# Storing only the inner sums of the nested second product's weights

## Chip, cores and metric

The kernel runs on one core of one Trainium2 chip. The metric is the device time of one execution in microseconds (us), lower is better. All data is fp32. Five engines work side by side, each through its own instructions in order: TensorE (PE, matmuls), VectorE (DVE), ScalarE (ACT), GpSimd (POOL) and SyncE (SP), which here only issues transfers (DMAs).

## The reference, cut

```python
# q, k, v: (4, 8, 768, 64); lam: (8,); domain_probs: (3072, 4); w1: (4, 512, 1024); w2: (4, 1024, 512)
for b in range(12):                       # blocks of 64 positions, per batch and head
    intra = (qb @ kb.T * Dmask) @ vb      # Dmask[i, j] = lam ** (i - j) for i >= j
    out[b] = intra + (qb * lam_pow) @ kv_state
    kv_state = lam_block * kv_state + (kb * rev_pow).T @ vb
x = out.transpose(0, 2, 1, 3).reshape(3072, 512)
p = domain_probs / (domain_probs.sum(-1, keepdims=True) + 1e-09)
y = sum(p[:, e:e+1] * (relu(x @ w1[e]) @ w2[e]) for e in range(4))
```

A block-wise decayed linear attention makes `x`; then four experts, each two matrix products with a relu between them, weighted by a gate per token.

## The kernel before

The 3072 tokens are cut into three groups of 1024, and a unit is one expert on one group. Unit order: group 0 with experts 0, 1, 2, 3, then groups 1 and 2 with experts 2, 3, 0, 1 each, so twelve units, numbered 0 to 11.

Each of the two products of a unit is done by a Strassen-like scheme of 2 x 2 blocks with seven products M1 to M7. A product's operand is a plain block of the weights (A11, A12, A22 for M1, M2, M4) or a sum of blocks (S1 to S4 for M5, M6, M7, M3). The first product of units 1 to 11, and the second product of units 4 to 11, are *nested*: each of the seven products is itself cut in 2 x 2 and done with seven inner products, whose operands are again three plain quarters (A11, A12, A22) and four inner sums (S3, S2, S1, S4). The second products of units 0 to 3 are plain, as is unit 0's first. The loop body of unit k runs the second product of unit k beside the first product of unit k + 1, piece by piece; units 4 to 11 are called the nested units.

Weights are prepared while the products run. `prepare_w1` and `prepare_w2` return lists of small jobs, *chores*: load blocks of the weights (`block`), form an outer sum on POOL (`total`, two 128x512 operations, stored to DRAM as `w2_sums`), form the four inner sums of one operand on POOL (`inner`, `inner_w2`, four 128x256 operations, tile `ops`) and store the operand to DRAM (`w1_ops`, `w2_ops`). For w2 this is done either together with the outer sums (`prepare_w2(e, both=True)`, experts 2 and 3) or later by `prepare_w2_ops(e)` (experts 0 and 1), which fetches an operand back (`w2f`), sums and stores. `w2_ops[e, m]` holds seven 256-wide entries an operand: A11, S3, S2, A22, S1, A12, S4. Six stores write them (L339). `feed3` (L1124) loads them for the product, in four loads of 256, 256, 256 and 128 KB into a ring of six `w2t` tiles; in the last unit one 896 KB load an operand goes to a tile `w2s`.

The order of everything is written out when the program is made. A count of steps `now` advances by one for each of eight parts of a product; `pump` takes the next chore when a modelled POOL is free (`free`, `busy`), with a factor PACE per unit between the chores; stores of results are held back by `store` for two steps after the modelled end of the sums, and put on SP. Until unit 4 begins, chores use tiles of a ring of seven `stage` tiles (tag "st"); at the start of unit 4 all chores that are left are forced out in one go:

```python
        if at == NEST:
            while chores:
                pump(force=True)
            chores.extend(prepare_w2_ops(0) + prepare_w2_ops(1))
            spare.append(True)
```

All else goes over the same engines in the same order lists: the attention of groups 1 and 2 runs inside units 0 to 3 (`turn`, `scores`, `values`). `values` gathers x in pairs of tiles `xc` (from the ring `small` of 42 tiles of 128x512, which also gives `m`, `to`, `gb`, `kv`, `st` and others, in turn). `pair_sums` forms four sums of them on POOL (tile `to`, L102) and SP stores both to `x_blocks` (L788 to L791). `x_fill` (L386) loads these as `xs`, the moving operand of the first product. `feed` loads that product's weights `ws_in` (L928 to L930, L932). For the last third of the attention, q and k are turned by 128 small DRAM-to-DRAM copies of 32 KB (`across`, L435), trickled out one by one on SP; before a batch is loaded back (`qx`, `kx`, L451), all its remaining copies are issued at once. `w2t` loads of the plain second products are at L1051; TensorE's matmuls are at L1018 (first product), L1072 (plain second) and L1362 (nested second); `out` stores of group 0 are at L1092. Nearly all DVE and POOL additions go through one helper, L102.

Places in the program are given below by *matmul numbers*: how many 128x256 matmuls stand ahead in TensorE's order. Unit 0 begins at 112, units 1, 2, 3 at 322, 532, 742, and unit 4 at 952. The profile records each such matmul as two.

Of the kernel before, what the change touches and what calls it, by code (L numbers as in the profile page):

```python
# [21 lines left out]
def kernel(  # L22
# [69 lines left out]
    def small(name):  # L92
        return pool.tile([P, W], FP32, name=name, tag="t")

    def acc_tile(name):
        return opool.tile([P, W], FP32, name=name, tag="acc")

# [64 lines left out]
    w1_ops = dram.tile([E, 7, P, 7, 256], FP32, name="w1_ops")  # L162
    x_blocks = dram.tile([NG - 1, P, 4, 7, 256], FP32, name="x_blocks")
    w2_sums = dram.tile([E, 4, P, 4, DH], FP32, name="w2_sums")
    w2_ops = dram.tile([E, 7, P, 7, 2, P], FP32, name="w2_ops")

    W1_AT = {n: i for i, n in enumerate(("M1", "M7", "M6", "M5", "M3", "M2", "M4"))}
    X_AT = {"M1": 0, "M5": 1, "M2": 2, "M3": 3, "M7": 4, "M6": 5, "M4": 6}
# [7 lines left out]
    def store(f):  # L176
        queue.append((busy[0] + (8 if spare else 2), f))
# [152 lines left out]
    def inner_w2(e, m, blk, two):  # L330
        b = {f"A{i + 1}{j + 1}": blk[j][:, :, i * P:(i + 1) * P] for i in range(2) for j in range(2)}
        s = [x.rearrange("p c d -> p (c d)").rearrange("p (k c d) -> p k c d", k=2, c=2) for x in two("ops")]
        for name, x, y, op in S_OPS:
            b[name] = s[SLOT[name] // 2][:, SLOT[name] % 2]
            tt(nc.gpsimd, b[name], b[x], b[y], op)
        to = w2_ops[e, MS.index(m)]
        b["S3"] = s[0]
        at = (("A11", 0), ("S3", slice(1, 3)), ("A22", 3), ("S1", 4), ("A12", 5), ("S4", 6))
        store(lambda: ([nc.sync.dma_start(out=to[:, x], in_=b[n]) for n, x in at], made.add(("w2", e, m))))  # L339

    def prepare_w2_ops(e):

        def two(name):
            return [small(name)[:].rearrange("p (c d) -> p c d", c=2) for _ in range(2)]

        st = {}

        def fetch(m):
            st[m] = two("w2f")
            for x in range(2):  # L350
                nc.sync.dma_start(out=st[m][x], in_=w2_form(e, A_OF[m])[:, 2 * x:2 * x + 2])

        def ready(m):
            inner_w2(e, m, st.pop(m), two)

        return [
            lambda: fetch(SEQ3[0]), pause(4),
            *(lambda i=i: (i < 6 and fetch(SEQ3[i + 1]), ready(SEQ3[i])) for i in range(7)),
        ]
# [173 lines left out]
    gate_bc = {}  # L533

    def spread_gates(g, e):
        gate_bc[unit_of[g, e]] = two = [small("gb")[:].rearrange("p (n t) -> p n t", t=P) for _ in range(2)]
        for j, t in enumerate(two):
            src = gate_rows[g - 1, 4 * j:4 * j + 4, e]
            nc.scalar.dma_start(out=t, in_=src.partition_broadcast(P))
# [239 lines left out]

    def pair_sums(g, x, o):  # L780

        s = [small("to") for _ in range(2)]
        (b12, b11), (b22, b21) = ((t[:, 0:256], t[:, 256:512]) for t in o)
        t1, t2, t3, t4 = (t[:, i * 256:(i + 1) * 256] for t in s for i in range(2))
        for to, a, b in ((t1, b12, b11), (t2, b22, t1), (t3, b22, b12), (t4, b21, t2)):
            tt(nc.gpsimd, to, a, b, ALU.subtract)
        store(lambda: (
            nc.sync.dma_start(out=x_blocks[g - 1, :, x, 0], in_=b11),  # L788
            nc.sync.dma_start(out=x_blocks[g - 1, :, x, 1:3], in_=o[1][:].rearrange("p (i t) -> p i t", i=2)),
            *(  # L790
                nc.sync.dma_start(out=x_blocks[g - 1, :, x, 3 + 2 * y:5 + 2 * y], in_=t[:].rearrange("p (i t) -> p i t", i=2))  # L791
                for y, t in enumerate(s)
            ),
            made.add(("blocks", g, x)),
        ))
# [308 lines left out]
    def feed3(e, m, k):  # L1104

        x_e = units[e][1]
        until(("w2", x_e, m))
        if e == FINAL and m != SEQ3[0]:

            if k == 0:  # L1110
                t = xp.tile([P, 7, 256], FP32, name="w2s", tag="x" + SEQ[SEQ3.index(m)])
                if (e, m) == PLAIN:
                    i, j = int(A_OF[m][1]) - 1, int(A_OF[m][2]) - 1
                    src = moe_w2[x_e, j * W:(j + 1) * W, i * DH:(i + 1) * DH]
                    nc.sync.dma_start(out=t[:, 0:4], in_=src.rearrange("(k p) d -> p k d", p=P))
                    fed3[e, m, 0] = t
                    return
                nc.sync.dma_start(out=t[:], in_=w2_ops[x_e, MS.index(m)].rearrange("p k c d -> p k (c d)"))
                for x in range(4):
                    fed3[e, m, x] = t[:, 2 * x:min(2 * x + 2, 7)]  # L1120
            return
        t = w2pool.tile([P, 2, DH], FP32, name="w2t", tag="w2")
        n = min(2, 7 - 2 * k)
        nc.sync.dma_start(  # L1124
            out=t[:, 0:n], in_=w2_ops[x_e, MS.index(m), :, 2 * k:2 * k + n].rearrange("p k c d -> p k (c d)"),
        )
        fed3[e, m, k] = t

# [94 lines left out]
    def plain_product(e, m, tags):  # L1225
        def part(dd, t):
            if t == 0:
                banks.append(bank(tags[dd], "p" + m))
            p = banks[dd]
            for q in range(2):  # L1230
                for c in range(2):
                    nc.tensor.matmul(
                        out=p[:, t * 256:(t + 1) * 256], lhsT=fed3[e, m, 0][:, 2 * q + c, dd * P:(dd + 1) * P],
                        rhs=outer[e][B_OF[m]][f"{q + 1}{t + 1}"][:, c * 256:(c + 1) * 256],
                        start=(t == 0 and q == 0 and c == 0), stop=True, skip_group_check=True,
                    )
            if t == 1:
                o = sums[m][:, 2 * dd:2 * dd + 2].rearrange("p k t -> p (k t)")
                tt(nc.vector, o, p[:], o, ALU.add)

        banks = []
        none = lambda: None
        return [f for dd in range(2) for t in range(2) for f in (lambda dd=dd, t=t: part(dd, t), none)]
# [17 lines left out]
    def turned_product(t, h, w):  # L1261
        p, o = ends[t], small("y")
        for s in range(2):
            for c in range(2):
                nc.tensor.matmul(
                    out=p[:, s * P:(s + 1) * P], lhsT=h[:, c * 256 + s * P:c * 256 + (s + 1) * P],
                    rhs=w[:, c * P:(c + 1) * P], start=False, stop=True, skip_group_check=True,
                )
        nc.scalar.copy(out=o[:, 0:256], in_=p[:, 0:256])
        i, j = RESULT[END[1]]  # L1270
        r = token(LAST, j, 2 * t)
        nc.sync.dma_start(
            out=out[r:r + 256, i * DH:i * DH + P].rearrange("(s p) d -> p s d", p=P),
            in_=o[:, 0:256].rearrange("p (s d) -> p s d", s=2),
        )
# [66 lines left out]
    def nested_product(e, m, tags):  # L1342
# [8 lines left out]

        def inner(x, i):
            if (e, m) == END and i in ("M2", "M3"):
                turned_product(("M2", "M3").index(i), b[B_OF[i]], fed3[e, m, x // 2][:, x % 2])
                return
            t = tags[0] if i in ("M1", "M6", "M5", "M3") else tags[1]
            fresh = i in ("M1", "M7", "M2")
            if fresh:
                banks[t] = bank(t, "p" + t)
            p = banks[t]  # L1360
            for c in range(2):
                nc.tensor.matmul(  # L1362
                    out=p[:, 0:256], lhsT=fed3[e, m, x // 2][:, x % 2, c * P:(c + 1) * P],
                    rhs=b[B_OF[i]][:, c * 256:(c + 1) * 256], start=(fresh and c == 0), stop=True,
                    skip_group_check=True,
                )
            at, begins = READ[i]
            o = sums[m][:, BLOCKS.index(at)]
            if begins and e in (NEST, 2 * E):
                nc.scalar.copy(out=o, in_=p[:, 0:256])  # L1370
            else:
                tt(nc.vector, o, p[:, 0:256], o, ALU.add)
            if (e, m, i) == (*END, "M5"):
                o = sums[m][:, BLOCKS.index("12")]
                tt(nc.vector, o, p[:, 0:256], o, ALU.add)
# [239 lines left out]
    for g in range(1, NG):  # L1615
        attention(g)
    steps.insert(0, (12, turn_gates))
    PACE = 1.15, 1.15, 1.4, 1.4, 1.3, 1.3, 1.3, 1.4, 1.0, 1.0, 1.0, 1.0
    first_steps = first_result()
    for at, (g, e) in enumerate(units):  # L1620
        if at == 0:
            chores.extend(prepare_w1(3) + prepare_w2(2, True) + prepare_w2(3, True) + prepare_w1(0))
        ahead = units[at + 1] if at + 1 < len(units) else None
        nested, nests = at >= NEST, ahead and at + 1 >= NEST
        if at == NEST:
            while chores:
                pump(force=True)
            chores.extend(prepare_w2_ops(0) + prepare_w2_ops(1))
            spare.append(True)
        blocks, banks = {}, {}  # L1630
        for i in range(7):
# [108 lines left out]
```

## Time and profile before

| | |
|---|---|
| median of 3 runs | 1242.48 us (1240.96 to 1244.87) |
| profiled execution | 1239.18 us, span 1237.3 us |
| mean granted TensorE clock | 0.975 of full speed |
| PE busy | 1158.7 us (94%), 7983 records |
| DVE / POOL / ACT busy | 842.6 (68%) / 826.3 (67%) / 316.2 us (26%) |
| transfers | 267.23 MB, 296153 packets, 216 GB/s over the span |
| chain that ended last | PE 77%, DVE 10%, DMA 5%, SP's queue 4%, POOL 1% |

Times within the span are counted from its first instruction. Windows give the busy microseconds of each engine inside a stretch; PEclk is the share of the clock that TensorE was granted; the DMA share is how busy the 16 DMA engines were on average. In a timeline the bracket names how long the engine had been idle before an instruction and which event ended that wait. "SPq" is SP issuing transfers, `w_ops` stands for `w1_ops` or `w2_ops`, `w_sums` for `w2_sums`.

### The profile page before, as it was taken

What the parts mean: (1) busy time and instruction counts of PE and PEld (TensorE: products, weight loads), DVE (VectorE), ACT (ScalarE), POOL (GpSimd) and SP (SyncE); (2) the same over time, 40 slices, a digit from 0 to 9 for tenths busy, and PEclk for the clock granted to TensorE, in tenths of its full rate; (3) what the DMA queues carried; (4) which work ended last, traced back from release to release, by engine and by line L of the source; (5) the groups of instructions that cost most, each with busy time, mean ns of one, the idle gap of its engine ahead of it and who ended that gap; (6) DMA issues with size and microseconds to landing.
All of it is one profiled execution on the core that took longest, in us unless ns stands there. A gap on an engine that the chain in (4) does not pass through costs nothing.

```text
span 1237.3 us, 21855 instructions
## 1 busy us (share of the span) xinstructions
PE 1158.7 (94%) x7983; PEld 998.1 (81%) x7983; DVE 842.6 (68%) x1525; ACT 316.2 (26%) x638; POOL 826.3 (67%) x768
## 2 busy tenths in 40 slices
PE   8999899999789984689899999999999999999998
PEld 7888788888667874577788888888887888888877
DVE  4688785775357643567457777788976667786785
ACT  4321122023101210112234234123234252242322
POOL 2856267758372644678669789898485585593884
PEclk9999999999889998799899999999999999999999
DMA  8876549999798985965498778885555665655562
GB/s 190 220 224 197 179 145 300 283 306 279 243 292 269 287 243 138 303 197 176 130 304 276 228 249 257 269 251 185 183 152 168 201 195 159 191 153 179 161 210 68
DMA packets 296153, 267.23 MB, mean 216 GB/s; under 512 B 140464, under 2 KB 236272, under 8 KB 296048
## 3 DMA queue, kind: packets, MB, share of 16 engines
q1 hardware_dynamic: 281088, 260.91, 68.9%
q10 hardware_dynamic: 14960, 4.94, 1.8%
q8 instruction: 64, 1.05, 0.3%
q14 instruction: 41, 0.34, 0.1%
HBM read 194.96 MB, written 75.01 MB: 218 GB/s over the span
## 4 chain that ended last, share of the span: by engine, by line
PE 77%; DVE 10%; DMA 5%; SPq 4%; POOL 1%; issue 1%; ACT 0%; ACTq 0%; DVEq 0%; POOLq 0%
PE pg L1018 33%; PE pq L1362 24%; PE q L1072 12%; DVE m L102 4%; PE pM L1464 2%; SPq L435 2%; DVE hT L102 1%; DVE sums L102 1%; DVE xs L102 1%; PE pc L1464 1%; DMA ws_in<-w_ops 1%; PE sp L676 1%; PE op L730 1%; DMA across<-in_k_dram 1%; PE op L748 1%
## 5 line engine op out<-in xcount | busy, mean ns | idle before, releaser
L1018 PE MATMUL pg<-xs,ws_in 128*128 128x256 f32 x1960 | 479.5, 385 | 20.5 <-DMA ws_in<-w_ops 11.5
L1018 PEld LDWEIGHTS pg<-xs,ws_in 128*128 128x128 f32 x1960 | 374.4, 193 | 79.7 <-issue 12.8
L102 DVE TENSOR_TENSOR m<-pg,m 128x512 f32<-128x512 f32 x451 | 307.7, 687 | 145.2 <-PE pg L1018 111.2
L102 POOL TENSOR_TENSOR m<-m,gb 128x512 f32<-128x512 f32 x128 | 167.2, 1325 | 97.5 <-ACT m L1030 71.6
L1072 PE MATMUL q<-w2t,m 128*128 128x256 f32 x896 | 220.4, 390 | 5.9 <-DVE m L102 5.9
L1072 PEld LDWEIGHTS q<-w2t,m 128*128 128x128 f32 x896 | 173.5, 195 | 31.9 <-DVE m L102 6.7
L1362 PE MATMUL pq<-acc,w2t 128*128 128x256 f32 x800 | 198.1, 381 | 0.2 <-DVE sums L102 0.2
L102 DVE TENSOR_TENSOR sums<-pq,sums 128x256 f32<-128x256 f32 x321 | 133.0, 420 | 86.1 <-PE pq L1362 74.1
L1362 PEld LDWEIGHTS pq<-acc,w2t 128*128 128x128 f32 x800 | 152.2, 191 | 22.0 <-issue 1.1
L1030 ACT ACTIVATE m<-m 128x512 f32<-128x512 f32 x132 | 83.0, 630 | 238.3 <-DVE m L102 233.1
L1089 DVE SCALAR_TENSOR_TENSOR acc<-q,gate,acc 128x256 f32<-128x256 f32 x96 | 46.2, 481 | 94.9 <-PE q L1072 94.5
L102 POOL TENSOR_TENSOR acc<-hT,hT 128x512 f32<-128x512 f32 x64 | 82.7, 1306 | 41.1 <-PE pq L1362 39.1
L1026 ACT COPY m<-pg 128x512 f32<-128x512 f32 x88 | 51.5, 586 | 173.4 <-PE pg L1018 165.2
L102 POOL TENSOR_TENSOR acc<-hT,acc 128x512 f32<-128x512 f32 x64 | 84.9, 1327 | 12.7 <-PE pq L1362 7.6
L102 DVE TENSOR_TENSOR m<-m,m 128x512 f32<-128x512 f32 x96 | 81.5, 851 | 11.9 <-DMA x_blocks<-xc 6.0
L1362 PE MATMUL pq<-hT,w2t 128*128 128x256 f32 x336 | 86.3, 379 | 0.1
L102 POOL TENSOR_TENSOR xs<-xs 128x256 f32<-128x256 f32 x40 | 31.8, 796 | 67.3 <-DMA xs<-x_blocks 64.5
L1362 PEld LDWEIGHTS pq<-hT,w2t 128*128 128x128 f32 x336 | 63.7, 190 | 9.1 <-DVE sums L102 0.5
L1362 PE MATMUL pq<-m,w2t 128*128 128x256 f32 x264 | 69.2, 385 | 1.7 <-DVE xc L102 1.6
L951 ACT COPY up<-m 128x512 f32<-128x512 f32 x56 | 32.5, 588 | 124.9 <-DVE m L102 124.7
L102 POOL TENSOR_TENSOR acc<-m,acc 128x512 f32<-128x512 f32 x44 | 57.0, 1295 | 3.2
L1362 PEld LDWEIGHTS pq<-m,w2t 128*128 128x128 f32 x264 | 50.2, 192 | 10.0 <-ACT xc L769 1.7
(143 smaller groups left out, 1336.6 us busy)
## 6 DMA issues: line engine op xcount, KB each, us to landing
w2t<-w_ops SPq DMA_DIRECT2D x150, 256.0 KB, 3.5
ws_in<-w_ops SPq DMA_DIRECT2D x40, 896.0 KB, 7.2
ws_in<-w_ops SPq DMA_DIRECT2D x30, 512.0 KB, 5.6
w_ops<-ops SPq DMA_DIRECT2D x28, 512.0 KB, 4.8
w_sums<-w2o SPq DMA_DIRECT2D x16, 512.0 KB, 4.3
w2t<-w_sums SPq DMA_DIRECT2D x32, 256.0 KB, 4.3
ws_in<-in_moe_w_dram SPq DMA_DIRECT2D x30, 256.0 KB, 5.7
w_ops<-ops SPq DMA_DIRECT2D x28, 256.0 KB, 4.4
```

Source lines behind the costliest of these rows:

```text
L102: eng.tensor_tensor(out=o, in0=a, in1=b, op=op)
L435: pieces.append((b, lambda to=to, src=src: nc.sync.dma_start(out=to, in_=src.rearrange("(t p) d -> p t d", p=32),)))
L676: nc.tensor.matmul(out=sp[r][half[x], ac * BL:(ac + 1) * BL], lhsT=hc(kT)[half[r], ac, blk[x]], rhs=hc(qT)[half[r], ac, blk[x]], start=(ac ...
L730: nc.tensor.matmul(out=op[r][half[y], cols(a, r) if x == r else apart(a)], lhsT=state[half[r], x, 2 * a + y], rhs=by_block(qs)[half[r], 2 ...
L951: nc.scalar.copy(out=there[at][:], in_=a[at][:])
L1018: nc.tensor.matmul(out=p[:, j * 256:(j + 1) * 256], lhsT=ws[i][:, j * P:(j + 1) * P], rhs=xs[i], start=(fresh and j == 0), stop=True, skip ...
L1026: nc.scalar.copy(out=new[at][:], in_=p[:])
L1030: nc.scalar.activation(out=new[at][:], in_=new[at][:], func=AF.Relu)
L1072: nc.tensor.matmul(out=p[:, s * DH:(s + 1) * DH], lhsT=h[at][:, c * 256 + s * P:c * 256 + (s + 1) * P], rhs=fed2[g, e, m][x][:, c], start= ...
L1089: nc.vector.scalar_tensor_tensor(out=o, in0=x, scalar=w, in1=o, op0=ALU.mult, op1=ALU.add)
L1362: nc.tensor.matmul(out=p[:, 0:256], lhsT=fed3[e, m, x // 2][:, x % 2, c * P:(c + 1) * P], rhs=b[B_OF[i]][:, c * 256:(c + 1) * 256], start= ...
L1464: nc.tensor.matmul(out=p[:, s * 256:(s + 1) * 256], lhsT=a[c][:, f:f + P], rhs=b[:, c, j * 256:(j + 1) * 256], start=(s == 0 and c == 0 an ...
```

## The change

1. `w2_ops` keeps only the four inner sums of an operand (S3, S2, S1, S4), written by two stores of 256 KB instead of six. `feed3` reads the plain quarters where they are: in the weights themselves, or in `w2_sums` (`w2_form`). An operand is again four loads: A11's quarter (128 KB, rows of 512 bytes), S3 with S2, A12 with A22, S1 with S4. In the last unit an operand is four loads instead of one.
2. Expert 2 loses `both=True`: its outer sums alone are prepared early, its inner sums by `prepare_w2_ops(2)`, later, from fetched operands. The chores of `prepare_w2_ops` for experts 2, 0, 1 are queued at unit 0, behind all others, and run before unit 4 as far as pacing lets them; the forced flush at unit 4 is gone.
3. Until unit 4 begins, the gate tiles `gb`, the x sums `to` and the tiles of `prepare_w2_ops` come from the `stage` ring instead of the `small` ring (`twice`).
4. PACE is 1.0 for 1.15 in units 0 and 1, and 1.3 for 1.4 in units 2 and 3.

```diff
+    def twice(name):
+        if spare:
+            return [small(name)[:] for _ in range(2)]
+        t = stage.tile([P, 2, W], FP32, name=name, tag="st")
+        return [t[:, i] for i in range(2)]
...
-    w2_ops = dram.tile([E, 7, P, 7, 2, P], FP32, name="w2_ops")
+    w2_ops = dram.tile([E, 7, P, 4, 2, P], FP32, name="w2_ops")
...
-        b["S3"] = s[0]
-        at = (("A11", 0), ("S3", slice(1, 3)), ("A22", 3), ("S1", 4), ("A12", 5), ("S4", 6))
-        store(lambda: ([nc.sync.dma_start(out=to[:, x], in_=b[n]) for n, x in at], made.add(("w2", e, m))))
+        store(lambda: ([nc.sync.dma_start(out=to[:, 2 * q:2 * q + 2], in_=s[q]) for q in range(2)], made.add(("w2", e, m))))
...
         def two(name):
-            return [small(name)[:].rearrange("p (c d) -> p c d", c=2) for _ in range(2)]
+            if spare:
+                return [small(name)[:].rearrange("p (c d) -> p c d", c=2) for _ in range(2)]
+            t = stage.tile([P, 4, DH], FP32, name=name, tag="st")
+            return [t[:, 0:2], t[:, 2:4]]
...
-        gate_bc[unit_of[g, e]] = two = [small("gb")[:].rearrange("p (n t) -> p n t", t=P) for _ in range(2)]
+        gate_bc[unit_of[g, e]] = two = [t.rearrange("p (n t) -> p n t", t=P) for t in twice("gb")]
...
-        s = [small("to") for _ in range(2)]
+        s = twice("to")
...
+        ops, form = w2_ops[x_e, MS.index(m)].rearrange("p k c d -> p k (c d)"), w2_form(x_e, A_OF[m])
...
+            pieces = t[:, 6], t[:, 0:2], t[:, 4:6], t[:, 2:4]
+            ks = range(4)
+        else:
+            t = w2pool.tile([P, 2, DH], FP32, name="w2t", tag="w2")
+            pieces = {k: t[:, 0] if k == 0 else t}
+            ks = [k]
+        for k in ks:
+            x = pieces[k]
             if k == 0:
+                x = x.rearrange("p (c d) -> p c d", c=2)
+                nc.sync.dma_start(out=x, in_=form[:, 0:2, 0:P])
+                w["M1"] = [x[:, c] for c in range(2)]
+                continue
+            nc.sync.dma_start(out=x[:], in_={1: ops[:, 0:2], 2: form[:, 2:4], 3: ops[:, 2:4]}[k])
...
-    PACE = 1.15, 1.15, 1.4, 1.4, 1.3, 1.3, 1.3, 1.4, 1.0, 1.0, 1.0, 1.0
+    PACE = 1.0, 1.0, 1.3, 1.3, 1.3, 1.3, 1.3, 1.4, 1.0, 1.0, 1.0, 1.0
...
-            chores.extend(prepare_w1(3) + prepare_w2(2, True) + prepare_w2(3, True) + prepare_w1(0))
+            chores.extend(prepare_w1(3) + prepare_w2(2) + prepare_w2(3, True) + prepare_w1(0))
+            for x in (2, 0, 1):
+                chores.extend(prepare_w2_ops(x))
...
         if at == NEST:
-            while chores:
-                pump(force=True)
-            chores.extend(prepare_w2_ops(0) + prepare_w2_ops(1))
+            assert len(chores) < 20
             spare.append(True)
```

More of the change, by code (lines that the diff above doesn't have):

```diff
@@ L790, in pair_sums @@
             *(
-                nc.sync.dma_start(out=x_blocks[g - 1, :, x, 3 + 2 * y:5 + 2 * y], in_=t[:].rearrange("p (i t) -> p i t", i=2))
+                nc.sync.dma_start(out=x_blocks[g - 1, :, x, 3 + 2 * y:5 + 2 * y], in_=t.rearrange("p (i t) -> p i t", i=2))
                 for y, t in enumerate(s)
@@ L1107, in feed3 @@
         until(("w2", x_e, m))
+        w = fed3.setdefault((e, m), {})
+        ops, form = w2_ops[x_e, MS.index(m)].rearrange("p k c d -> p k (c d)"), w2_form(x_e, A_OF[m])
         if e == FINAL and m != SEQ3[0]:
-            if k == 0:
[L1111 to L1127, printed above, removed]
+            if k:
+                return
+            t = xp.tile([P, 7, 256], FP32, name="w2s", tag="x" + SEQ[SEQ3.index(m)])
+            if (e, m) == PLAIN:
+                nc.sync.dma_start(out=t[:, 0:4], in_=form)
+                w[0] = t
+                return
@@ new lines, in feed3 @@
+            pieces = t[:, 6], t[:, 0:2], t[:, 4:6], t[:, 2:4]
[6 more added lines that the diff above has]
+            x = pieces[k]
+            if k == 0:
+                x = x.rearrange("p (c d) -> p c d", c=2)
[3 more added lines that the diff above has]
+            nc.sync.dma_start(out=x[:], in_={1: ops[:, 0:2], 2: form[:, 2:4], 3: ops[:, 2:4]}[k])
+            if k == 2:
+                w["M2"], w["M4"] = ([x[:, c, y * P:(y + 1) * P] for c in range(2)] for y in range(2))
+            else:
+                for y, i in enumerate({1: ("M7", "M6"), 3: ("M5", "M3")}[k]):
+                    w[i] = [x[:, y, c * P:(c + 1) * P] for c in range(2)]
@@ L1232, in part @@
                     nc.tensor.matmul(
-                        out=p[:, t * 256:(t + 1) * 256], lhsT=fed3[e, m, 0][:, 2 * q + c, dd * P:(dd + 1) * P],
+                        out=p[:, t * 256:(t + 1) * 256], lhsT=fed3[e, m][0][:, 2 * q + c, dd * P:(dd + 1) * P],
                         rhs=outer[e][B_OF[m]][f"{q + 1}{t + 1}"][:, c * 256:(c + 1) * 256],
@@ L1266, in turned_product @@
                     out=p[:, s * P:(s + 1) * P], lhsT=h[:, c * 256 + s * P:c * 256 + (s + 1) * P],
-                    rhs=w[:, c * P:(c + 1) * P], start=False, stop=True, skip_group_check=True,
+                    rhs=w[c], start=False, stop=True, skip_group_check=True,
                 )
@@ L1353, in inner @@
             if (e, m) == END and i in ("M2", "M3"):
-                turned_product(("M2", "M3").index(i), b[B_OF[i]], fed3[e, m, x // 2][:, x % 2])
+                turned_product(("M2", "M3").index(i), b[B_OF[i]], fed3[e, m][i])
                 return
@@ L1362, in inner @@
                 nc.tensor.matmul(
-                    out=p[:, 0:256], lhsT=fed3[e, m, x // 2][:, x % 2, c * P:(c + 1) * P],
+                    out=p[:, 0:256], lhsT=fed3[e, m][i][c],
                     rhs=b[B_OF[i]][:, c * 256:(c + 1) * 256], start=(fresh and c == 0), stop=True,
```

## Prediction

> **What bounds the kernel now.** I read the page first (engines and slices), then the table by stage, then TensorE's gaps, then what DVE and the SP queue did inside the largest gap. PE is busy 1158.7 of 1237.3 us, so at most 78.6 us of gaps can be won, and the slices say where they lie:
>
> ```profile
> PE   8999899999789984689899999999999999999998
> POOL 2856267758372644678669789898485585593884
> PEclk9999999999889998799899999999999999999999
> ```
>
> A slice is 30.9 us. PE and its clock dip together in slices 10 to 19, the second half of the plain units. The stage table (units 0, 1, 2, 3, then the nested units):
>
> ```profile
> core 0: us, PE busy (x) PEld busy (x) DVE busy (x) ACT busy (x) POOL busy (x), PEclk, DMA share, GB/s
> 88.50:194.00 105.50, 100.72 (x767) 87.00 (x767) 83.16 (x138) 19.61 (x39) 58.91 (x60) 1.00 0.58 178
> 194.00:298.00 104.00, 104.00 (x963) 90.07 (x962) 72.26 (x130) 21.80 (x48) 78.82 (x90) 1.00 0.94 294
> 298.00:411.50 113.50, 98.06 (x823) 81.78 (x822) 62.78 (x113) 16.14 (x38) 58.27 (x66) 0.92 0.88 265
> 411.50:573.00 161.50, 124.20 (x1068) 104.73 (x1067) 85.50 (x148) 21.08 (x48) 97.54 (x106) 0.89 0.74 224
> 573.00:1237.00 664.00, 648.96 (x3092) 563.64 (x3090) 481.97 (x860) 208.57 (x393) 485.71 (x405) 0.99 0.64 199
> ```
>
> Unit 1 is full. Unit 2 has 15.4 us of gaps and loses 0.08 x 98 = 7.8 us to the clock; unit 3 has 37.3 us and loses 0.11 x 124 = 13.7. The nested units have 15 us in 664, mostly the tail. So the change is decided between 298 and 600 us. TensorE's timeline there names what ended each gap (in brackets):
>
> ```profile
> 324.45 3.75 PE L1018 MATMUL pg<-xs,ws_in 128*128 128x256 f32 x8 [6.49 <-DMA ws_in<-w_ops]
> 365.17 3.78 PE L1018 MATMUL pg<-xs,ws_in 128*128 128x256 f32 x8 [4.21 <-DVE m L102]
> 381.29 2.07 PE L1072 MATMUL q<-w2t,m 128*128 128x256 f32 x4 [2.59 <-DVE m L102]
> 448.65 2.83 PE L1018 MATMUL pg<-xs,ws_in 128*128 128x256 f32 x8 [4.43 <-DMA ws_in<-w_ops]
> 502.35 0.48 PE L730 MATMUL op<-qs,kv 64*64 64x64 f32 x4 [22.82 <-DVE kv L102]
> 592.34 0.69 PE L730 MATMUL op<-qs,kv 64*64 64x64 f32 x32 [3.26 <-DVE kv L102]
> ```
>
> I call the first A, the next two B, then C and D. A and C wait for first-product weights. B and D wait for DVE, and DVE for a buffer: its own timeline, then SP's, inside D:
>
> ```profile
> 499.68 0.69 DVE L102 TENSOR_TENSOR m<-pg,m 128x512 f32<-128x512 f32 x1 [21.55 <-DMA x_blocks<-xc]
> ```
>
> ```profile
> 466.46 8.22 SPq L435 DMA_DIRECT2D across<-in_q_dram  x11
> 474.73 10.40 SPq L435 DMA_DIRECT2D across<-in_k_dram  x16
> 492.43 0.43 SPq L929 DMA_DIRECT2D ws_in<-w_ops  x1
> 493.44 0.64 SPq L788 DMA_DIRECT2D x_blocks<-xc  x1
> ```
>
> DVE wants an `m` tile whose buffer still holds `xc`; the store of `xc` stands on SP behind 27 small copies (18.6 us), then loads. Every one of these gaps goes back to SP's single queue being late, none to POOL's or DVE's total.
>
> **The change part by part.** TensorE's and ACT's orders are the same in both programs, DVE's differs in three moved steps, POOL has the same 762 operations. SP has 1045 transfers instead of 1128 (260.8 to 253.5 MB): 84 stores of plain blocks (0.47 to 0.6 us of SP each) go, 28 partial stores are merged, 14 fetches and 15 split loads are added. Expert 2's seven inner operands move from units 1 and 2 into unit 3, expert 0's seven from the nested units to the end of unit 3. Per unit, SP issues and MB: unit 1 132 and 31.6 to 132 and 32.6; unit 2 169 and 34.9 to 124 and 30.8; unit 3 140 and 28.9 to 169 and 36.0.
>
> A: the table above charges 6.49 us, the 0.99 us before it (a wait for POOL's `kn`) and slow matmuls. Eight records (four matmuls) take 1.73 us at full clock, 0.432 us a matmul; after the gap they took 3.75 and 2.75, so 3.0 us more: 10.5 in all. In the changed order that `ws_in` issue stands at matmul 540 instead of 561, 21 x 0.432 = 9.1 us earlier, and between matmuls 546 and 588 SP has 28 issues for 50. That covers the gap, but unit 1 sends 1.1 MB more into a DMA share of 0.94, so I take -8; bounds 0 and -10.5.
>
> (The Trainium skill, "TensorE: Matmul & The Clock Gate", section "The HAM clock gate", has the clock at half for one window of about 3.4 us after an idle one, which would lose 1.7 us, not the 3.0 of these rows; by it A and B are each 1.3 us smaller and the forecast 2.6 us later.)
>
> B: 4.21, 0.95 in the gaps just before and after, 2.59, and 3.2 + 1.9 us of slow matmuls: 12.8. DVE waited at matmul 629 for an `xc` store standing at 624. `to` tiles now come from the stage ring, the rotation of the 42 small buffers is slower, and the wait is at 625 to 627 for a store at 608: 17 x 0.432 = 7.3 us of lead against 2.2. I take -9; bounds 0 and -12.8.
>
> C: 4.43, 1.4 in two earlier `ws_in` waits, 2.1 slow: 7.9. The `ws_in` issue moves only from 762 to 757, but six stores ahead of it (SP 432.4 to 436.9 us) become four. -3; bounds +2 and -7.9.
>
> D: the 27 copies stay where they were, so the gap stays. What goes is DVE's wait at 834: in the new order that `m` tile waits for an old `vn`, and it is an ACT copy of the next `xc` at 836 that waits for the store. DVE's `kv` and the attention product are then done inside the gap, and PE resumes when `ws_in` (issued 492.4, median 5.6 to land) arrives, about 498.5, instead of at 505.2. Two `w2f` loads now stand ahead of it (+1.2); the store ahead of the copies that waits for POOL (2.9 us on SP) has 2.5 us less POOL work before it. -7; bounds +2 and -10 (with the 2.67 us `kx` wait at 520 that is DVE catching up).
>
> New in unit 3: between matmuls 866 and 952 POOL gets 48.2 us of work instead of 25.8 (seven groups of four 0.73 us sums of expert 0, which before waited for unit 4 or later), and SP 63 issues instead of 35. Before, that stretch lasted about 40 us (537 to 577). POOL's gates and inner sums stand behind the groups, and the first nested product waits for the last `acc` (562.5 to 565 before, needed near 574). So 9 us of slack there, 5.6 us of waits for ACT that the groups can fill, and 48.2 - 40 = 8 us too many: I take +4; bounds 0 and +22.4. Behind POOL stand the stores of those sums on SP, and behind them `ws_in` and `w2t`.
>
> Nested units: reading plain blocks in place replaces one for one (four `w2t` loads an operand, one of them in 512-byte runs); PE is full there and SP waits for PE 233 us, so loads have that much lead. POOL, at up to 24.7 of 25 us between 650 and 850, has seven groups fewer. 0; bounds -3 and +3.
>
> (Against it, "DMA: Bandwidth & Descriptors", section "Why small descriptors are slow", counts about 3 fixed cycles a packet; 512-byte instead of 2 KB runs would then cost, by estimate, 13% more engine time on 7 MB. No run here shows it, and the DMA share there is 0.64.)
>
> PACE 1.0 for 1.15 in units 0 and 1 moves chores a few matmuls forward; POOL has 17 us a unit free. 0.
>
> Sum: -8 - 9 - 3 - 7 + 4 = -23. The profiled execution took 1239.18 us (span 1237.3 + 1.9), 3.3 below the median of 1242.48. 1239.18 - 23 = 1216.2, and at the median's level 1219.5.
>
> **The rivals.** *Bandwidth, not order.* Unit 1 runs 294 GB/s at a share of 0.94, and up to matmul 546 the change moves 2.2 MB more (73.5 for 71.2): 7.6 us at that rate, nearly A's whole lead. Then A, B and C stay and only D and the late POOL work count: -3, about 1239.5. For it: the share. Against: in unit 1 PE never waited at that share.
>
> *POOL late at the end of unit 3 (slower).* Place: POOL, matmuls 866 to 952. If nothing absorbs the groups, 22.4 us show; a `ws_in` on SP behind a store that waits for POOL adds its 7.2 us landing, and the clock 3.0: +32.6 against the -27 won, +5.6, 1248. It decides once the first nested product starts over 27 us behind the weights. Against: the bounded slack above.
>
> *All of it.* If SP is never late before D and reaches the copies 5 us earlier, every bound is met without the POOL cost: about -40, 1202.
>
> That the change doesn't do what it says is ruled out by the program: the stores are gone, TensorE's order is unchanged.
>
> **How the numbers follow.** Forecast (1210 to 1230) 0.56, bandwidth 0.18, POOL late 0.14, all of it 0.12. A run of this kernel tells 0.3% (3.7 us) from no change: below 1238.8 is faster, above 1246.2 slower. Faster: 0.56 + 0.12 + half of bandwidth 0.09 + 0.01 = 0.78; same 0.10; slower 0.12. Leaving out about 0.06 below and 0.12 above gives 1203 to 1246.
>
> **What would show it.** Right: unit 2 near 100 us long with its clock above 0.97; no DVE wait for `x_blocks<-xc` over 2 us; D still there, 15 to 19 us, ended by `ws_in`; POOL over 22 of 25 us in the last 40 us of unit 3. Wrong: A still over 4 us with a DMA share at 0.95 (bandwidth); PE waiting for POOL `acc` or `m` at the first nested product by over 10 us (POOL late); D gone.

## The result, and the profile after

| | median, us | ratio to before, 95% interval |
|---|---|---|
| before | 1241.72 (4 runs, 1239.69 to 1244.87) | |
| changed | 1222.28 (4 runs, 1221.54 to 1223.5) | 0.9842 [0.9819, 0.9865] |

The change gains 19.4 us. The profiled execution took 1223.5 us (span 1221.7, mean granted clock 0.976), 15.7 less than the one of before. The forecast of 1219.5 was 2.8 us off. That closeness flatters it: several steps behind it were wrong and cancelled, and the experiments show which.

The page's slices for the changed kernel, 30.5 us each:

```profile
PE   8999898999999995786999999999999999999998
POOL 2857158777766752998679688686585584693884
PEclk9999999999999997897899999999999999999999
```

Counted from 0, the dips of PE and its clock that lay in slices 10 to 19 are gone from 10 to 14; those from slice 15 on remain. There is a new small one, the 8 in slice 6. The stage table of the changed kernel (units 0, 1, 2, 3, nested units; columns as in the prediction's table):

```profile
88.20:200.40 112.20, 103.47 (x767) 89.08 (x766) 81.32 (x138) 19.62 (x39) 62.87 (x67) 0.97 0.57 178
200.40:307.10 106.70, 105.47 (x966) 90.51 (x965) 77.70 (x130) 21.61 (x48) 81.35 (x86) 1.00 0.96 299
307.10:415.60 108.50, 105.09 (x989) 90.11 (x988) 75.88 (x130) 19.45 (x46) 74.56 (x82) 0.98 0.94 290
415.60:556.90 141.30, 108.98 (x901) 91.95 (x901) 74.56 (x131) 17.91 (x40) 96.23 (x113) 0.89 0.84 266
556.90:1221.70 664.80, 650.54 (x3089) 565.20 (x3088) 481.53 (x859) 208.60 (x393) 468.67 (x379) 0.99 0.57 180
```

One boundary in the prediction's own table was wrong: it cut between units 2 and 3 at 411.5 us, 14.7 us too early. By the first L1072 matmul of unit 3 the kernel before stands thus:

```profile
298.40:426.20 127.80, 112.36 (x989) 93.97 (x989) 72.52 (x129) 19.44 (x46) 69.26 (x79) 0.93 0.90 269
426.20:573.60 147.40, 110.10 (x902) 92.64 (x901) 76.09 (x131) 17.79 (x40) 86.78 (x92) 0.88 0.71 215
```

The two tables give the difference by unit: unit 0 +6.8 us (105.4 to 112.2), unit 1 +2.2 (104.5 to 106.7), unit 2 -19.3, unit 3 -6.1, nested units +1.1. Units 2 and 3, where the gain was expected, brought it, and units 0 and 1, priced at nothing, cost 9 us. TensorE's gaps in the changed kernel, from its timeline, answer to A to D:

```profile
197.43 1.13 PE L690 MATMUL sp<-vn,kn 64*64 64x64 f32 x32 [4.51 <-POOL kn L108]
363.93 3.11 PE L1025 MATMUL pg<-xs,ws_in 128*128 128x256 f32 x8 [2.07 <-DVE m L108]
372.40 1.13 PE L1079 MATMUL q<-w2t,m 128*128 128x256 f32 x4 [1.34 <-DVE m L108]
476.26 4.01 PE L1025 MATMUL pg<-xs,ws_in 128*128 128x256 f32 x8 [12.44 <-DMA ws_in<-in_moe_w_dram]
555.05 2.07 PE L1025 MATMUL pg<-xs,ws_in 128*128 128x256 f32 x4 [8.46 <-DVE m L108]
576.76 1.13 PE L737 MATMUL op<-qs,kv 64*64 64x64 f32 x32 [5.18 <-DVE kv L108]
```

A (324) and C (448) are gone. Of B two short waits are left. D is 12.44 us and ends with `ws_in`, as forecast. The first and the last two rows are new or larger: POOL is late there. SP inside D still stands behind the batch of small copies, with two `w2f` loads (0.98 us) between them and `ws_in`:

```profile
445.06 7.38 SPq L442 DMA_DIRECT2D across<-in_q_dram  x10
452.48 10.40 SPq L442 DMA_DIRECT2D across<-in_k_dram  x16
...
467.11 0.98 SPq L358 DMA_DIRECT2D w2f<-w_sums  x2
...
472.35 0.34 SPq L935 DMA_DIRECT2D ws_in<-in_moe_w_dram  x1
```

### The profile page after: what moved, and what is told of

It reads as the page before. It is cut to its first block, busy times and chain, and to the rows that moved or that the text cites. A ratio compares the mean times of both kernels' runs of the same rounds, so it can differ in the third digit from the quotient of the medians.

```text
span 1221.7 us, 21731 instructions
## 1 busy us (share of the span) xinstructions
PE 1157.0 (95%) x7983; PEld 998.0 (82%) x7983; DVE 845.4 (69%) x1525; ACT 316.0 (26%) x638; POOL 830.1 (68%) x768
## 4 chain that ended last, share of the span: by engine, by line
PE 47%; DVE 4%; DMA 1%; issue 0%; SPq 0%; ACT 0%; DVEq 0%
PE pq L1379 24%; PE pg L1025 22%; DVE sums L108 1%; DVE m L108 1%; DMA w2s<-w_ops 1%; DVE hT L108 1%; DVE xs L108 1%; PE pg L1379 0%; PE pM L1249 0%; PE yp L1209 0%; SPq L1139 0%; PE yp L1282 0%; DVE y L1230 0%; ACT m L1037 0%; SPq L1136 0%
## 5 line engine op out<-in xcount | busy, mean ns | idle before, releaser
L108 POOL TENSOR_TENSOR acc<-hT,acc 128x512 f32<-128x512 f32 x64 | 84.9, 1326 | 12.7 <-PE pq L1379 7.6
L108 DVE TENSOR_TENSOR m<-m,m 128x512 f32<-128x512 f32 x96 | 86.2, 901 | 3.7 <-PE q L1079 3.7
```

Source lines behind the costliest of these rows:

```text
L108: eng.tensor_tensor(out=o, in0=a, in1=b, op=op)
```

## The experiments

Theory: SP's single queue sets units 2 and 3, and the change wins by lightening and rearranging it; what it gives back comes from POOL's order, in unit 0 through PACE and at the end of unit 3 through the early operands of experts 0 and 1. Rivals: the new gaps are a by-product of SP's lateness, the ring rotation is what matters, or bytes do and not issues. Each group of four kernels has a median of before of its own, 1241.3 to 1243.0 us. Times of whole kernels are medians of four runs; the lengths of units and gaps come from one profiled execution of each.

### 1. PACE of unit 0 (changed kernel, one number)

```diff
-    PACE = 1.0, 1.0, 1.3, 1.3, ...
+    PACE = 1.15, 1.0, 1.3, 1.3, ...
```

> The changed kernel with the old PACE of 1.15 in unit 0 alone. In the changed kernel TensorE waits 4.51 us at 197 us for POOL's kn, which stands behind one more pair of w1 sums than before; unit 0 lasts 112.2 us instead of 105.4. Theory (the moved chore is the cause): the wait goes, unit 0 is back at 105 to 106 us, and the whole is 5 to 7 us faster than the changed kernel, near 1216. Rival (the time is only taken up by the next wait): the 4.5 us come back in units 1 and 2, where the DMA share is over 0.9, and the whole stays within 2 us of 1222.

Measured: 1216.53 us (1210.67 to 1218.79), 0.9775 [0.9739, 0.981], 5.8 less than the changed kernel. In the profile, which is of the fastest of the four runs, unit 0 is back at 105.4 us. Part of the cost moved on: unit 1 is 2.9 us longer, with a wait of 2.44 us for `kn`. Unit 3 is 8.7 us shorter in this execution. POOL's timelines show why. The changed kernel, then the kernel before, at the same place of the program:

```profile
193.30 2.48 POOL L108 TENSOR_TENSOR w1o<-w1o,w1b 128x512 f32<-128x512 f32 x2 [2.48 <-DMA w_ops<-w1o]
...
196.32 1.06 POOL L108 TENSOR_TENSOR kn<-kn,decay 128x512 f32<-128x512 f32 x1
```

```profile
191.19 1.06 POOL L102 TENSOR_TENSOR kn<-kn,decay 128x512 f32<-128x512 f32 x1
194.15 2.50 POOL L102 TENSOR_TENSOR w1o<-w1o,w1b 128x512 f32<-128x512 f32 x2 [1.89 <-PE pg L1018]
```

With PACE 1.0 a pair of outer sums, waiting 2.48 us for a buffer whose store is in flight, slips in ahead of `kn`, for which TensorE then waits 4.51 us. POOL is idle 49 of the 112 us of unit 0; its total says nothing here, its order does.

### 2. Experts 0 and 1 held back until unit 4

```diff
-            for x in (2, 0, 1):
-                chores.extend(prepare_w2_ops(x))
+            chores.extend(prepare_w2_ops(2))
...
-            assert len(chores) < 20
+            assert not chores
+            chores.extend(prepare_w2_ops(0) + prepare_w2_ops(1))
```

> The changed kernel with expert 0's (and 1's) inner sums queued only when unit 4 begins, as before the change; expert 2's are made as in the change. It takes seven groups of sums (about 20 us) off POOL between matmuls 866 and 952. Theory (POOL late at the end of unit 3): the 8.46 us gap at 555 us, where TensorE waits for DVE and DVE 9.4 us for POOL's m, goes and the whole is 7 to 11 us faster than the changed kernel, near 1213. Rival (the gap is the DVE chain's, POOL only fills it): the gap stays over 5 us and the whole within 3 us of 1222.

Measured: 1211.61 us (1210.62 to 1214.28), 0.974 [0.9714, 0.9766], 10.7 less. Unit 3 is 130.1 us for 141.3, the gap near 555 is gone, and the nested units are no longer for it (663.9 against 664.8). So making the seven operands of expert 0 at the end of unit 3 costs 10.7 us and buys nothing later. Not all of that need be POOL's: the edit also takes 30 of SP's 169 issues out of unit 3, and D is 9.87 us for 12.44. The chain behind the gap, DVE's timeline in the changed kernel:

```profile
553.30 1.09 DVE L108 TENSOR_TENSOR hT<-m,m 128x512 f32<-128x512 f32 x1 [9.36 <-POOL m L108]
```

and the busy time between 525 and 575 us, POOL the fifth engine of the row:

```profile
525.00:550.00 25.00, 19.11 (x188) 16.34 (x188) 11.58 (x21) 3.30 (x9) 24.30 (x28) 0.98 0.95 332
550.00:575.00 25.00, 16.53 (x108) 13.63 (x108) 19.56 (x24) 5.70 (x11) 24.53 (x19) 0.82 0.61 198
```

POOL is full for 50 us, the gates `m` queue behind `ops`, DVE behind the gates, TensorE behind DVE.

### 3. The x sums and gates back in the small ring

```diff
     def twice(name):
-        if spare:
-            return [small(name)[:] for _ in range(2)]
-        t = stage.tile([P, 2, W], FP32, name=name, tag="st")
-        return [t[:, i] for i in range(2)]
+        return [small(name)[:] for _ in range(2)]
```

> The changed kernel with the x sums and gates back in the ring of 42 small tiles; all else as changed. Theory (rotation of the ring is what took DVE's waits away in B and D): a wait of DVE for x_blocks<-xc of 10 us or more is back inside the long gap near 460 to 485 us, the gap is ended by DVE's kv and not by ws_in and is 5 to 8 us longer, B stays short since SP is earlier there; the whole is 5 to 9 us slower than the changed kernel, near 1229. Rival (SP's order alone sets the gap, DVE's wait lies inside it): within 3 us of 1222.

Measured: 1222.87 us (1221.13 to 1223.39), 0.9831 [0.9808, 0.9854]: no difference. The buffer wait came back all the same, in DVE's timeline:

```profile
476.61 0.69 DVE L105 TENSOR_TENSOR m<-pg,m 128x512 f32<-128x512 f32 x1 [17.07 <-DMA x_blocks<-xc]
```

D is 18.39 us then and named after DVE, instead of 12.44 named after `ws_in`; but units 2 and 3 take 107.0 and 140.4 us against 108.5 and 141.3. The name and length of one gap changed and the time did not: work that is not done inside the gap follows it, and the other way round. My theory of the ring rotation, worth 5 to 9 us, fell.

### 4. Copies across partitions earlier

Two more small copies per product in units 0 to 2, so that the batch of 26 ahead of D's `ws_in` goes:

```diff
                 if x % 2:
                     trickle()
+                if at in (0, 1, 2) and x in (2, 6):
+                    trickle()
```

> The changed kernel with two more of the 32 KB copies issued per product in units 0 to 2, so that 2 and not 26 stand on SP ahead of the last batch; the same copies in all. Theory (SP's queue, not DVE, POOL or bandwidth, sets D): the 12.44 us wait for ws_in at 476 us goes to under 3 us, with its slow matmuls, and the whole is 10 to 15 us faster than the changed kernel, near 1210. Rival (bandwidth): the copies' 128-byte pieces take DMA time from units 1 and 2, which are at a share of 0.91 to 1.00, and 5 us or more of new ws_in waits appear there; the whole is 0 to 8 us faster.

Measured: 1219.48 us (1217.2 to 1221.09), 0.9804 [0.978, 0.9829], only 2.8 less. D is gone and unit 3 takes 123.5 us for 141.3, which shows that the batch made it. But units 0, 1 and 2 are 2.1, 6.6 and 2.3 us longer. The theory was right about D and wrong about the whole. The rival has the size of the whole, but the new `ws_in` waits that it named did not come: there is one, of 1.51 us, in unit 2. The new wait in unit 1 is one of 2.97 us for POOL's `kn`. What makes these units longer is not shown; runs 8 and 9 take it up.

### 5 and 6. The two halves of the change, each alone

The stores: the changed kernel with the chores' order, PACE and flush of before.

```diff
-            chores.extend(prepare_w1(3) + prepare_w2(2) + prepare_w2(3, True) + prepare_w1(0))
-            for x in (2, 0, 1):
-                chores.extend(prepare_w2_ops(x))
+            chores.extend(prepare_w1(3) + prepare_w2(2, True) + prepare_w2(3, True) + prepare_w1(0))
...
-            assert len(chores) < 20
+            while chores:
+                pump(force=True)
+            chores.extend(prepare_w2_ops(0) + prepare_w2_ops(1))
...
+    PACE = 1.15, 1.15, 1.4, 1.4, ...
```

> The new operand layout alone: inner sums stored without the plain blocks and plain blocks read in place, but the order of the chores, their PACE and the flush before unit 4 are those of the kernel before (the stage tiles stay, since the small tiles cost nothing). Theory 'fewer stores': the five stores that each nested operand no longer queues on SP are what frees units 2 and 3; unit 2 falls from 127.8 us to about 110, unit 3 from 147.4 to 135-142, unit 0 stays at 105.4, and the whole is 1218-1226 us, as the changed kernel or better. Rival 'order': what frees unit 2 is that expert 2's nested operands are made later; then unit 2 stays above 120 us and the whole is 1233-1242 us. Halfway (1227-1232 us) the two share the gain.

The order: the kernel before with the opposite edit and the stage tiles, all six stores an operand kept.

> The other half alone: the order of the chores, PACE and stage tiles of the changed kernel, but every nested operand is stored whole, plain blocks too, with six stores each, as before. Theory 'fewer stores': unit 2 is freed in part, since expert 2's seven operands leave it, and the stores come back in unit 3, where they stand ahead of unit 3's weights: unit 2 112-118 us, unit 3 150-160, whole 1238-1248 us. Rival 'order': unit 2 falls to about 108 us and unit 3 to about 141, whole 1221-1230 us. Unit 0 is 112 us under both, since PACE sets it.

Measured: the stores alone 1207.79 us (1205.7 to 1209.39), 0.9743 [0.9697, 0.9789]; the order alone 1256.44 us (1255.06 to 1258.39), 1.0135 [1.0095, 1.0174]. So fewer stores win 33.5 us and the new order loses 15.1; the sum, -18.4, is close to the -19.4 of the change. The stores did better than their theory's 1218 to 1226 us; the order alone lies above both of its ranges, with unit 2 at 126.1 and unit 3 at 155.5 us. TensorE's gaps with the order alone:

```profile
325.67 1.96 PE L1027 MATMUL pg<-xs,ws_in 128*128 128x256 f32 x8 [1.76 <-DMA ws_in<-w_ops]
347.95 3.67 PE L1027 MATMUL pg<-xs,ws_in 128*128 128x256 f32 x8 [7.81 <-DMA ws_in<-w_ops]
585.31 2.07 PE L1027 MATMUL pg<-xs,ws_in 128*128 128x256 f32 x4 [18.99 <-DVE m L108]
```

A's wait of 6.49 us falls to 1.76, as the order's lead had it, and a wait of 7.81 us stands 22 us later: with the stores still there SP is late at another matmul. The last row, 18.99 us, is at the place of the rival "POOL late", priced at 22.4. But POOL is not full there: it is busy 38.4 us between 535 and 587, and in that stretch waits 5.8 us for fetched operands (`w2f`) and 6.0 us for their stores. So transfers stand behind this gap as well. With the stores alone the rows that answer to them are these; A is 4.05 us, D 10.84, the gap at the end of unit 3 absent, and unit 2 takes 114.7 us and unit 3 127.6:

```profile
322.58 3.12 PE L1025 MATMUL pg<-xs,ws_in 128*128 128x256 f32 x8 [4.05 <-DMA ws_in<-w_ops]
473.91 3.41 PE L1025 MATMUL pg<-xs,ws_in 128*128 128x256 f32 x8 [10.84 <-DMA ws_in<-in_moe_w_dram]
```

### 7. Both corrections together

The edits of 1 and 2 on the changed kernel.

> The changed kernel with the two corrections together: PACE of unit 0 back at 1.15, and the nested operands of experts 0 and 1 queued only when unit 4 begins. If the two costs are separate they add: 1222.3 - 5.8 - 10.7 = 1205.8 us, with unit 0 at 105.4 and unit 3 at 125-131. Rival: both act through the same reserve, how far POOL is behind as unit 3 ends; alone the first already cut the gap there from 8.5 to 4.9 us, so together they give only some 12 us: 1209-1211 us.

Measured: 1209.58 us (1209.27 to 1210.06), 0.9755 [0.9712, 0.9798]. That is 12.7 us together, not 16.5, and in the rival's range. That a POOL less far behind and a POOL with less to do are partly the same slack fits, but is not shown: run 1 alone spread over 8.1 us, so the plain sum is not excluded. What is left of the new order, expert 2's operands made later and the PACE of units 1 to 3, is worth nothing over the stores alone: 1209.6 against 1207.8, unit 1 longer (110.4 us for 104.5), unit 2 shorter (109.1 for 114.7). In unit 1, where PACE is still 1.0, POOL again forms a pair of w1 sums ahead of `kn`, after 6.29 us of waiting for a buffer, and TensorE waits 3.23 us for `kn`. That wait is absent in the stores alone (PACE 1.15) and in the changed kernel (1.0 in both units). No run changes PACE in unit 1 alone, so its cause stays open.

### 8, 9 and 10. Copies earlier where the DMA engines are free

Two more copies per product in unit 0 alone (DMA share 0.57), on top of 7, then on top of the stores alone; the third, also on the stores alone, has four more per product in place of two.

```diff
+                if at == 0 and x in (2, 6):      # third: (0, 2, 4, 6)
+                    trickle()
```

> The same with 14 extra copies of q and k across partitions in unit 0 alone, where the DMA engines are busy 57% of the time against 95% in units 1 and 2, so that some 12 of 26 copies are left in the batch ahead of unit 3's weights. Theory (SP's queue sets the gap near 476 us, and the extra copies cost time only where the DMA engines are full): the gap falls by 12-14 x 0.6 us, some 6 us, units 1 and 2 stay within 1 us of the run without the copies, and the whole is 4-6 us below that run, about 1200 us. Rival (a copy costs what it saves wherever it stands): unit 0 or 1 is longer by as much, and the whole is within 2 us of the run without the copies.

> The new operand layout alone (old order and PACE, 1207.8 us) with the 14 extra copies of q and k in unit 0. Theory: the 10.84 us gap ended by ws_in near 474 us goes, with the slow matmuls behind it, as it did on top of the other version (-12.2 us there): 1195-1198 us. Rival: in the old order the copies meet other stores in unit 2 (114.7 us, DMA engines 93% busy) and come out even: 1204-1208 us.

> The same with 28 extra copies in unit 0, so that no batch is left. Theory: once the gap is gone there is nothing more to win in unit 3; units 1 and 2 are as with 14: within 2 us of that run. Rival: each copy taken out of units 1 and 2 frees 0.6 us of SP there and shortens the rest of the wait at 322 us (4.05 us) and the one at 370 us: 3-6 us less.

Measured: 1197.39 us (1194.78 to 1200.22), 0.9658 [0.9618, 0.9697]; 1201.17 us (1198.28 to 1202.17), 0.9672 [0.9658, 0.9686]; 1201.1 us (1198.94 to 1202.44), 0.9674 [0.9659, 0.9688]. The first gained 12.2 us over 7, twice what I had worked out: 14 copies in the batch for 27 close the whole gap of 6.98 us that 7 still had there, and the slow matmuls and the catching up behind it go too (unit 3 119.8 for 127.1 us, clock 0.94 for 0.92). The second gained 6.6 over the stores alone, between theory and rival: unit 3 is 10.7 us shorter, units 1 and 2 together 3.5 longer. The third is the second within 0.1 us, so beyond the closed gap there is nothing more to win from the copies. All three beat both kernels; their intervals overlap, so no order among them is claimed.

### 11 and 12. Issues or bytes

To the stores alone, behind the two stores of an operand: four tiny ones (issues of before, bytes of the new layout), or the same two again elsewhere (bytes of before and a seventh more, four issues for six).

```diff
+   [nc.sync.dma_start(out=more[e, MS.index(m), x, 0:1, 0, 0], in_=s[x % 2][0:1, 0, 0]) for x in range(4)],   # 11
+   [nc.sync.dma_start(out=more[e, MS.index(m), x], in_=s[x]) for x in range(2)],                             # 12
```

> The new operand layout alone (1207.8 us), and behind the two stores of each nested operand four more of 512 bytes each: the number of SP's DMA issues is that of the kernel before, the bytes are the new ones. Theory 'SP's issue time': 14 operands in units 1 to 3 at 4 x 0.35-0.5 us are 20-28 us of SP, and the time goes back most of the way, 1225-1240 us, with unit 2 above 120 us. Rival 'bytes': 1207-1212 us, unit 2 at 115.

> The new operand layout alone (1207.8 us), and behind the two stores of each nested operand the same two again to another place: the bytes are those of the kernel before and a seventh more (8 blocks against 7), the issues 4 against 6. Theory 'SP's issue time': half the way back, 14 x 2 x 0.45 = 13 us of SP: 1215-1225 us. Rival 'bytes': all the way back and a little more, 1235-1245 us, with the DMA engines at 90% or more in unit 2 and unit 2 above 125 us.

Measured: 1231.23 us (1228.52 to 1234.67), 0.992 [0.9896, 0.9944], and 1225.63 us (1224.64 to 1228.74), 0.9877 [0.9862, 0.9892]. Four issues an operand that move almost nothing take back 23.4 of the 33.5 us, with the DMA share of 300 to 425 us at only 0.82:

```profile
300.00:425.00 125.00, 112.71 (x999) 95.23 (x998) 75.23 (x134) 19.73 (x47) 73.52 (x82) 0.93 0.82 248
```

SP's timelines show what an issue holds of the queue (start, length, how many): first two of the six stores of an operand in the kernel before, then the four tiny ones of run 11 at two places, then the two of 256 KB of run 12:

```profile
378.50 0.69 SPq L339 DMA_DIRECT2D w_ops<-w2o  x1
379.29 0.45 SPq L339 DMA_DIRECT2D w_ops<-ops  x1
```

```profile
321.08 4.86 SPq L345 DMA_DIRECT2D more<-ops  x4
...
378.08 1.18 SPq L345 DMA_DIRECT2D more<-ops  x4
```

```profile
375.59 0.94 SPq L345 DMA_DIRECT2D more<-ops  x2
```

That is 0.45 to 0.69 us a store of before, 0.3 us an issue of 512 bytes (1.18 / 4) and 0.47 us one of 256 KB (0.94 / 2). The row at 321.08 shows a second price. The four are held up there by a wait of 3.1 us for a `ws_in` load that they have nothing to do with. In these programs SP's transfers use eight semaphores (counters that tell when a transfer has landed) in turn, and each is issued only when the last transfer with the same semaphore has landed. Counted from the traces over units 2 and 3, such waits are 6.9 us with the stores alone and 17.6 us in run 11, and the issues themselves hold SP 173.0 and 186.9 us; the two units are 21.6 us longer. So more issues cost through both, and run 11 does not part them.

Run 11 fell within the issue theory's range, and run 12 0.6 us above it. Two full stores an operand cost 17.8 us, half as many issues three quarters of the price. If the price grows evenly with the issues, run 11 gives 5.9 us for one more issue per operand (23.4 / 4), two are 11.7 and some 6 us are left for bytes. By this estimate the number of issues is the larger part and bytes the smaller.

Counted from the traces, SP's transfers issued in units 2 and 3 against the length of these units:

| kernel | issues | us |
|---|---|---|
| order alone (6) | 381 | 281.6 |
| before | 312 | 275.2 |
| stores alone + 4 tiny stores (11) | 312 | 263.9 |
| changed | 299 | 249.8 |
| small ring (3) | 295 | 247.4 |
| PACE of unit 0 (1) | 294 | 241.5 |
| stores alone + 2 stores (12) | 288 | 258.4 |
| copies in units 0 to 2 (4) | 273 | 234.3 |
| experts 0 and 1 held (2) | 272 | 240.5 |
| both corrections (7) | 271 | 236.2 |
| stores alone (5) | 264 | 242.3 |
| 7 with copies (8) | 259 | 227.4 |
| stores alone with copies (9) | 250 | 232.9 |
| stores alone with more copies (10) | 236 | 229.7 |

From first to last that is 51.9 us for 145 issues, 0.36 us each. The order is not strict: 312 issues stand beside 275.2 and 263.9 us, and run 8, the shortest, has 23 issues more than run 10. So what else is in the two units, and at which place, counts as well.

## Why the prediction was right, and where not

**What bounds the kernel** held: SP's queue sets units 2 and 3. Runs 5, 8 and 11 show it from three sides, by fewer stores, by earlier copies, and by adding issues alone.

**A** was forecast at -8 and is gone in full (-10.5). The reason given, the issue standing 21 matmuls earlier, is only part: with the order alone another wait, of 7.81 us, stands at 347.95, and with the stores alone A keeps 4.05 of 6.49 us. In these runs only both together cleared it.

**B** (-9): two waits of 2.07 and 1.34 us are left of 4.21 and 2.59; with the slow matmuls some 7 to 8 us went. The size was right. The step that gave it, "`to` tiles now come from the stage ring, the rotation of the 42 small buffers is slower", fell with run 3.

**C** (-3) is gone, about -7: "six stores ahead of it become four" was sized too small, because it took the stores next to the wait and not SP's whole backlog. C is absent with the stores alone (run 5), and run 11 brings it back (4.16 us) by issues alone.

**D** (-7): from 22.82 us, ended by DVE, to 12.44 us ended by `ws_in`, plus 1.5 of a `kv` wait just before: -8.9, as described, with `ws_in` issued at 472.35 and used at 476.26. It is shorter than the 15 to 19 us named as a sign. But run 3 shows that the part won by freeing DVE's buffer is no gain of the unit. What counts in D is when SP reaches `ws_in`.

**New in unit 3** (+4, bounds 0 and 22.4) was mis-sized: the 10.7 us of run 2, SP's share in them included, lie in the bounds, near the middle. The "9 us of slack" were not there, since the gates `m` are needed all along the stretch and not only the last `acc` at its end. The rival "POOL late" had the right mechanism and place, with a gap of 8.46 us for 22.4; it did not decide, because more was won ahead of it. With the stores left in (run 6) the gap there is 18.99 us and the whole 1256 us, with SP's transfers late too.

**PACE** (0) was the step that failed outright. "POOL has 17 us a unit free" is an argument from a total, and even the total is not what the stage table gives, 46.6 and 25.2 us in units 0 and 1. What PACE moved was one pair of sums past `kn`. It cost unit 0 6.8 us in the trace, and the whole 5.8 us in the median.

**Nested units** (0, bounds ±3): +1.1 us, and -1.2 us with the stores alone, which has the same in-place reads. The cost that the Trainium skill's "DMA: Bandwidth & Descriptors" (section "Why small descriptors are slow") suggests for the 512-byte runs does not show there, with TensorE busy 650.5 of the 664.8 us.

**The clock after a gap.** By the prediction's estimate from the page "TensorE: Matmul & The Clock Gate" of the Trainium skill (section "The HAM clock gate"), one window at half clock loses 1.7 us; it priced 3.0 from the rows of before. From start to start, the two groups of eight records after the 12.44 us gap of the changed kernel took 5.86 us (476.26 to 482.12) against 3.46 at full clock, 2.4 us more, and the granted clock was 0.50 up to 480.70. After the 4.05 us gap of run 5 it was 1.8 us more, and for A of the kernel before, measured the same way, 2.9. So the loss differs from gap to gap, between the page's price and that of the rows.

**"Bandwidth, not order"** (1239.5) did not happen: A, B and C went while the DMA share rose to 0.96 and 0.94. **Summed up**, units 2 and 3 brought -25.4 us where the sum had -23, so the gains that were put too small paid for POOL; units 0, 1 and the nested ones cost 10.1 where the sum had nothing. That the total came out near is luck in that sense. In the profiled executions that is -15.7 for -23; that the medians differ by 19.4 is the spread of the runs.

The sign that unit 2 should be "near 100 us" came from the wrong boundary; it is 108.5 us, with its clock at 0.98.

## What to carry to other kernels

When one queue issues all transfers and runs late, count its issues before its bytes, and look at what each issue waits for: here two stores an operand instead of six won 33.5 us, and the new order of the same work alone lost 15.1. Price a reordering on an in-order engine by which instruction it moves ahead of one that somebody waits for, not by the idle share of that engine. And judge an edit by the length of the stage; a gap that changes its name or its length proves nothing.

## What was not expected of the hardware

Over units 1 to 3 a store of 512 bytes held SP's queue 0.26 us in the median of 56 (run 11), one of 256 KB 0.45 us in the median of 28 (run 12). With 512 times the bytes the time of an issue not even doubles. The spread at one size is wider: 0.21 to 0.92 us and 0.32 to 1.32 us. The small DRAM-to-DRAM copies of 32 KB, in pieces of 128 bytes, took 0.65 us each (10.40 us for 16), more than the store of 256 KB.
